# Gated linear recurrence and gated feed-forward on one core: one output projection step moved to the head of the later log passes

## The chip, the cores and the metric

The kernel runs on one core of a Trainium2 chip. The metric is the device time of one execution in microseconds (us); the median of 5 runs before the change is 286.07 us (284.23 to 286.88).

## The reference

Inputs q, k, v, a_re, a_im have shape (4, 8, 768, 48): batch, heads, sequence, head width. A complex decay (a_re, a_im), its magnitude held below 0.999, drives a recurrence; its real output y becomes the 3072 x 384 matrix x of a gated feed-forward.

```
S_re, S_im = (ar * S_re - ai * S_im + k v^T, ar * S_im + ai * S_re)
y[t] = q[t] @ S_re
...
g = x @ w_gate;  val = x @ w_val
ffn_out = (gelu(g) * val) @ w_out
out = x + sigmoid(x @ w_res) * ffn_out
```

w_gate and w_val are 384 x 1536, w_out is 1536 x 384, w_res is 384 x 384.

## The kernel before, in words

**Tiles and units.** The sequence is cut into 12 groups of 256 rows (two chunks of 128 rows, c = 0 and 1, all 8 heads, 384 columns). The groups g are numbered with the batch innermost, so groups 0 to 3 start the four sequences. They form seven units: [0], [1,2], [3,4], [5,6], [7,8], [9,10], [11]. A unit of two groups has 512 rows.

**Phases.** After a ramp (units 0 and 1 prepared), an outer loop over u calls `phase_x(u)`, here called log pass u, for u > 0, then `residuals()`, then `phase_y(u)`, then the loads for later units. Counted from u = 0, the passes with u >= 2 are "from the third on".

- *Log pass u* does, for the groups of unit u+1, the cumulative sums of the log magnitudes on TensorE (`cs_l`, matmuls of L272 named csl, float32), their exponentials E and Ei on ScalarE (L275, L276; reported as L144, the line of the helper `act`), the phase sums (`cs_t`, L291 and L293, named cst) with their reduction on VectorE (L295, L296, L301), and sines on ScalarE (`p2_sin`). For unit u+2 it does logarithms, exponentials (their product with a_im is L254 on VectorE) and arctangents. `decay2` sends rows of E and Ei through DRAM by GpSimd's queue (L345, L349, and L316 back); `multiply` (L361, VectorE, in phase y) makes of them the state's decay. Changes of ScalarE's function table are loads of their own (L642). It also holds the second half of the attention of unit u, and the output projection of unit u-1: one `op_step` per 128 rows, so four of them for a unit of two groups.
- *Phase y(u)* does the gate and value matmuls of unit u (`gv_step`, L595 gp and L599 vp, 12 steps), Gelu on ScalarE, the product of the two on VectorE (L602, into the tile h2), the residual gate (`rp_step`, L611), the products of the next unit's q and k with E and Ei and the sines (`products`, L369, L374, L381), and from its sixth tenth on the first half of the attention of unit u+1.

**Attention.** From group 3 on (`TURN`) Q and K are turned by transposing DMAs on SyncE's queue (L385, QT and KT). One attention step multiplies KT with QT (L446, named at), VectorE masks it (L449, atm), further steps are dk (L488), the state update and y (L496, L498), ScalarE casts y to x (L501), and `xt_step` transposes x on TensorE (L580, tpx).

**op_step (L615 to L631).** Twelve accumulating matmuls (L619) over the 12 slices of h2 into one PSUM tile; VectorE multiplies it with the residual gate into ot (L625); SyncE's queue writes ot to the output (L629). Later `residuals()` adds x to it by an accumulating DMA on GpSimd's queue (L637). A step needs all of h2, thus the last Gelu product of the phase y before.

**What sets the order.** `weave` gives each step of a stream a place between the stream's two ends (0 is the pass's start, 1 its end) and emits the steps in the order of these places. That is the program order; it becomes priority: a compile-time scheduler may issue a later step ahead of an earlier one that it takes to be not ready. On the chip each engine runs its instructions in the order so fixed, and each waits for its own semaphores. SyncE's queue takes, in this order around a pass: the transposes of the phase y before, then the loads of q, k, a_re, a_im for later units, then the writes of ot, then the next transposes.

**PSUM.** The pool psM has four one-bank buffers with one tag for csl, cst, op, gp, vp, rp and tpx, so at most four of these live at a time.

Of the kernel before, what the change touches and what calls it, by code (L numbers as in the profile page):

```python
# [17 lines left out]
def weave(*streams):  # L18

    order = []  # L20
    for si, (begin, end, steps) in enumerate(streams):
        n = len(steps)
        for i, step in enumerate(steps):
            order.append((begin + (end - begin) * (i + 0.5) / n, si, i, step))
    for _, _, _, step in sorted(order, key=lambda e: e[:3]):
        step()
# [3 lines left out]
def kernel(  # L30
# [181 lines left out]
    def squares(g):  # L212

        def q0():
            T["lm", g] = pS.tile([128, W], FP, tag="s", name="lm")
            with paced("gelu"):
                nc.scalar.activation(out=T["lm", g], in_=flat(T["ar", g]), func=AF.Square)

        def q1():
            if g < 5:  # L220
                if g == 0:
                    T["sq"] = hb.tile([128, 4, 2, DM], FP, tag="h2", name="sq0")
                t = T["sq"][:, g % 4].rearrange("p a m -> p (a m)")
            else:
                t = pE.tile([128, W], FP, tag="E", name="sq")
            T["sq", g] = t
            if g in DVSQ:
                nc.vector.tensor_tensor(out=t, in0=flat(T["ai", g]), in1=flat(T["ai", g]), op=OP.mult)
            else:
                with paced("gelu"):  # L230
                    nc.scalar.activation(out=t, in_=flat(T["ai", g]), func=AF.Square)  # L231

        def q2():
            with paced("gmul"):
                nc.vector._custom_dve(TENSOR_ADD_SAT, out=T["lm", g], in0=T["lm", g], in1=T["sq", g], s0=MAG2MAX, s1=0.0)  # L235
            if g in UNITS[2]:
                decay_raw(g)
        return [q0, q1, q2]

    def p1_steps(g):  # L240

        def s0():
            lm = T["lm", g]
            act(out=lm, in_=lm, func=AF.Ln)

        def s1():
            ar = flat(T["ar", g])
            T["s", g] = pE.tile([128, W], FP, tag="E" if g == 1 else "Ei", name="ra") if g in (1, 2) else ar
            act(out=T["s", g], in_=ar, func=AF.Ln)

        def s2():
            T["th", g] = flat(T["ai", g])
            act(out=T["s", g], in_=T["s", g], func=AF.Exp, scale=-1.0)
            nc.vector.tensor_tensor(out=T["th", g], in0=T["s", g], in1=T["th", g], op=OP.mult)  # L254
        return [s0, s1, s2]
# [5 lines left out]
    def cs_l(g, c):  # L261
        if c == 0:
            if g == 0:
                t = hb.tile([128, 4, DM], FP, tag="sg", name="E0")
                T["E", g] = t[:, 0:2].rearrange("p a m -> p (a m)")
                T["Ei", g] = t[:, 2:4].rearrange("p a m -> p (a m)")
            else:
                T["E", g] = pE.tile([128, W], FP, tag="E", name="E")
                T["Ei", g] = pE.tile([128, W], FP, tag="Ei", name="Ei")
        sl = slice(c * DM, (c + 1) * DM)  # L270
        cs = psM.tile([128, DM], FP, tag="mm", padded_shape=[128, 512], name="csl")
        nc.tensor.matmul(out=cs, lhsT=lmat[c], rhs=T["lm", g][:, sl], start=True, stop=True)  # L272

        def ex():
            act(out=T["E", g][:, sl], in_=cs, func=AF.Exp, scale=0.5)  # L275
            act(out=T["Ei", g][:, sl], in_=cs, func=AF.Exp, scale=-0.5)  # L276
        return ex
# [362 lines left out]
    def table(nm):  # L640
        def f():
            tab(nc.scalar.preload_act_table_set(nm))  # L642
        return f

    def gs(u):
        return UNITS[u] if 0 <= u < NU else []
# [7 lines left out]
    def call(f, *a):  # L654
        return lambda: f(*a)

    def zip_steps(lists):
        return [st[i] for i in range(max(map(len, lists), default=0)) for st in lists if i < len(st)]

    def att_steps(u, half):  # L660

        todo = [(g, c, i * C + c) for i, g in enumerate(gs(u)) for c in range(C)]
        n = len(todo) // 2
        steps = []
        for i, (g, c, jj) in enumerate(todo[half * n:half * n + n]):
            steps += attention(g, c)
            if i > 0:
                steps.insert(-1, call(xt_step, u, jj - 1))
        if n:
            steps.append(call(xt_step, u, half * n + n - 1))  # L670
        return steps

    def phase_x(u):

        pend = []
        g1 = gs(u + 1)
        p1g = [g for w in range(NU) if P1AT.get(w, w - 2) == u for g in gs(w)]
        now = [g for g in p1g if g in g1]
        ahead = [g for g in p1g if g not in g1]
        ops = [call(op_step, u - 1, jj) for jj in range(len(gs(u - 1)) * C)]  # L680
        att = att_steps(u, 1)
        if not g1:
            weave((0.0, 0.8, att), (0.1, 1.0, ops))
            return

        def csl(g, c):
            pend.append(cs_l(g, c))

        def ex():
            pend.pop(0)()  # L690

        def p1(g):
            st = p1_steps(g)[1:] if u < LAZY else p1_steps(g) + [call(decay0, g)]
            return (squares(g) if g == HELD else []) + st
        lns = [f for g in g1 for f in (p1_steps(g)[0], call(decay_exp, g))] if u <= LAZY else []
        csls = [call(csl, g, c) for g in g1 for c in range(C)]
        exs = [ex for _ in g1 for _ in range(C)]
        dec = [call(decay2, g) for g in g1]
        cst = [call(cs_t, g, c) for g in g1 for c in range(C)]
        sin = [call(p2_sin, g) for g in g1]  # L700
        table("natural_log_exp_and_others")()
        if now:
            atn = [table("trig_and_small")] + [call(p1_arctan, g) for g in now + ahead]
            pn = zip_steps([p1(g) for g in now])
            weave((0.0, 0.05, pn[:2]), (0.06, 0.1, csls), (0.12, 0.25, pn[2:]), (0.26, 0.4, exs),
                  (0.28, 0.48, zip_steps([p1(g) for g in ahead])),
                  (0.5, 0.5, dec), (0.55, 0.65, atn), (0.62, 0.8, cst), (0.9, 0.95, sin),
                  (0.0, 0.8, att), (0.0, 0.25, ops) if u == 1 else (0.1, 1.0, ops))
            return
        atn = [table("trig_and_small")] + [call(p1_arctan, g) for g in ahead]  # L710
        weave((0.0, 0.1, lns), (0.06, 0.16, csls) if lns else (0.0, 0.12, csls), (0.05, 0.5, zip_steps([p1(g) for g in ahead])), (0.12, 0.45, exs),
              (0.46, 0.46, dec), (0.2, 0.65, cst), (0.7, 0.95, atn + sin), (0.0, 0.8, att), (0.1, 1.0, ops))

    def ramp():

# [101 lines left out]
    for u in range(NU + 1):  # L817
        if u > 0:
            phase_x(u)
        if u == 1:  # L820
            with paced("turned"):
                for g in UNITS[3]:
                    decay_raw(g)
        residuals()
        phase_y(u)
        for g in gs(u + 2):
            with paced("turn"):
                load_q(g)
            after_landing(T["k", g], call(load_v, g))
        while T["a"] < (8 if u == 0 else min(NG, gs(u + 1)[-1] + 7 if gs(u + 1) else NG)):  # L830
            with paced("turn"):
                load_a(T["a"])
# [30 lines left out]
```

## Time and profile before

The profile is of one execution, whose own time was 286.39 us; its span on the core is 284.6 us, so 1.8 us lie around the span.

| what | measured |
|---|---|
| median of 5 runs, range | 286.07 us, 284.23 to 286.88 |
| profiled execution, its span | 286.39 us, 284.6 us |
| busy, TensorE / VectorE / ScalarE / GpSimd | 86% / 76% / 70% / 33% |
| L619 op: matmuls, busy | 288 (24 steps of 12), 50.7 us |
| L272 csl: idle of TensorE before it, in all | 11.4 us |
| log pass 2 (csl to the first gp) | about 107.1 to 126.0 us |
| log passes 3, 4, 5 begin their csl at | 147.0, 187.7, 225.2 us |
| write of one ot: KB, issue to landing | 192.0, 3.2 us |

Durations of single matmuls in the profile are latencies; twelve op matmuls in a row take 1.95 us on the chain (326 ns is the latency of one). "Idle" is the time an engine stood still before an instruction, with who ended the wait. PEclk is the granted share of TensorE's clock.

### The profile page before, as it was taken

The page shows a single profiled execution, that of the slowest core. Times are in us where ns is not written, and L with a number is a line of the kernel's source. Part 1 is how long each engine was busy: PE and PEld are TensorE (multiplying, and loading weights), DVE is VectorE, ACT ScalarE, POOL GpSimd, SP SyncE. Part 2 cuts the span into 40 slices and gives each one's busy share as a digit, 9 for nine tenths or more (in the row PEclk, how much of TensorE's full clock was granted, in tenths as well). Part 3 has the DMA queues.
Part 4 walks back from the last instruction along what each step waited for, and adds up shares of the span by engine and source line. Part 5 has one row for each costly group of instructions (what it writes and reads, how often), then busy time and mean ns, then how long its engine had stood idle before and what let it go on. Part 6 is the DMA issues. An engine that isn't in the chain of part 4 may idle for free.

```text
span 284.6 us, 5133 instructions
## 1 busy us (share of the span) xinstructions
PE 244.8 (86%) x1848; PEld 147.3 (52%) x1848; DVE 215.0 (76%) x376; ACT 198.8 (70%) x336; POOL 93.7 (33%) x141
## 2 busy tenths in 40 slices
PE   0435967997879969999999999989999998999993
PEld 0122645775434446554566544656545665456782
DVE  0669896995999575998878998869968587564453
ACT  4886898579994699885789866696655735455250
POOL 4021843130246402446604476024911242100220
PEclk9977586999999998999999999999999999999999
DMA  9999999999999999999999999999699486900631
GB/s 147 187 173 189 165 191 189 175 160 188 195 170 209 165 198 170 174 198 176 198 170 169 174 156 195 168 171 77 102 201 217 87 89 126 165 20 28 140 55 56
DMA packets 176001, 44.01 MB, mean 155 GB/s; under 512 B 165092, under 2 KB 175976, under 8 KB 175976
## 3 DMA queue, kind: packets, MB, share of 16 engines
q1 hardware_dynamic: 140744, 33.05, 70.6%
q0 software_dynamic: 35232, 10.64, 36.8%
q8 instruction: 14, 0.23, 0.3%
q14 instruction: 11, 0.09, 0.2%
HBM read 31.33 MB, written 9.08 MB: 142 GB/s over the span
## 4 chain that ended last, share of the span: by engine, by line
PE 64%; DMA 14%; DVE 7%; ACT 6%; SPq 5%; issue 2%; DVEq 0%
PE op L619 14%; PE gp L595 13%; PE vp L599 13%; DMA KT<-padK 8%; PE cst L291 5%; PE csl L272 5%; DMA q<-in_q_dram 5%; SPq L164 4%; PE at L446 2%; PE rp L611 2%; DMA ai<-in_a_im_dram 2%; PE tpx L580 2%; PE cst L293 2%; PE dk L488 1%; SPq L385 1%
## 5 line engine op out<-in xcount | busy, mean ns | idle before, releaser
L144 ACT ACTIVATE h<-gp 128x512 bf16<-128x512 f32 (+1 forms) x84 | 44.7, 536 | 38.1 <-PE gp L595 37.8
L602 DVE SCALAR_TENSOR_TENSOR h<-h,vp 128x512 bf16<-128x512 bf16 (+1 forms) x84 | 50.5, 608 | 20.3 <-PE vp L599 13.0
L595 PE MATMUL gp<-xT,wg 128*128 128x512 bf16 (+1 forms) x252 | 61.4, 352 | 1.5 <-ACT h L144 1.1
L599 PE MATMUL vp<-xT,wv 128*128 128x512 bf16 (+1 forms) x252 | 61.8, 352 | 0.5 <-ACT xT L584 0.4
L619 PE MATMUL op<-wo,h 128*128 128x384 bf16 x288 | 50.7, 326 | 1.4 <-ACT xT L584 1.3
L619 PEld LDWEIGHTS <-h 128*128 128x128 bf16 x288 | 27.3, 98 | 18.7 <-issue 2.5
L599 PEld LDWEIGHTS <-wv 128*128 128x128 bf16 x252 | 24.7, 99 | 22.9 <-issue 0.6
L316 POOL DMA_DIRECT2D m<-d x32 | 23.7, 778 | 37.1 <-DMA d<-Ei 17.1
L637 POOL DMA_DIRECT2D out_dram<-x x22 | 20.4, 1022 | 40.4 <-DMA out_dram<-ot 40.2
L595 PEld LDWEIGHTS <-wg 128*128 128x128 bf16 x252 | 23.6, 99 | 18.8 <-issue 1.7
L449 DVE TENSOR_TENSOR atm<-at,mask 128x512 bf16<-128x512 f32 x36 | 24.6, 684 | 8.8 <-PE at L446 8.8
L178 POOL DMA_DIRECT2D v<-in_v_dram x24 | 21.9, 919 | 17.7 <-DMA ai<-in_a_im_dram 12.2
L642 ACT ACT_TABLE_LOAD x21 | 26.9, 1283 | 1.1 <-PEq L847 0.7
L201 POOL COPY landed<-k 1x1 f32<-1x1 f32 x9 | 2.4, 267 | 64.3 <-DMA k<-in_k_dram 64.3
L272 PE MATMUL csl<-lm,lt0a 128*128 128x384 f32 x24 | 13.1, 637 | 11.4 <-ACT lm L144 11.4
L625 DVE SCALAR_TENSOR_TENSOR ot<-sg,op 128x384 f32<-128x384 f32 x24 | 13.2, 549 | 8.6 <-PE op L619 5.7
L291 PE MATMUL cst<-ai,ut0b 128*128 128x384 f32 x40 | 17.8, 537 | 0.1
L446 PE MATMUL at<-QT,KT 96*128 96x128 bf16 x144 | 14.4, 220 | 3.2 <-DMA KT<-padK 2.7
L235 DVE CUSTOM_DVE_ANT_0 lm<-lm,sq 128x768 f32<-128x768 f32 x12 | 11.4, 950 | 7.4 <-ACT sq L231 7.4
L144 ACT ACTIVATE ar<-ar 128x768 f32<-128x768 f32 x20 | 16.9, 851 | 0.1
L501 ACT CAST x<-y 128x384 bf16<-128x384 f32 x22 | 10.5, 478 | 8.9 <-PE y L498 8.5
L144 ACT ACTIVATE sg<-rp 128x384 f32<-128x384 f32 x24 | 11.6, 491 | 6.5 <-PE rp L611 5.4
(113 smaller groups left out, 459.1 us busy)
## 6 DMA issues: line engine op xcount, KB each, us to landing
ar<-in_a_re_dram SPq DMA_DIRECT2D x24, 192.0 KB, 5.0
ai<-in_a_im_dram SPq DMA_DIRECT2D x24, 192.0 KB, 5.0
q<-in_q_dram SPq DMA_DIRECT2D x24, 192.0 KB, 4.8
k<-in_k_dram SPq DMA_DIRECT2D x24, 192.0 KB, 5.1
out_dram<-ot SPq DMA_DIRECT2D x24, 192.0 KB, 3.2
out_dram<-x POOLq DMA_DIRECT2D x22, 192.0 KB, 5.6
v<-in_v_dram POOLq DMA_DIRECT2D x24, 96.0 KB, 5.1
wg<-in_moe_w_gate_dram POOLq DMA_DIRECT2D x4, 288.0 KB, 7.4
```

Source lines behind the costliest of these rows:

```text
L144: return tab(nc.scalar.activation(**kw))
L178: held(nc.gpsimd.dma_start(out=t[:, c], in_=rows(v, g, c)), after)
L272: nc.tensor.matmul(out=cs, lhsT=lmat[c], rhs=T["lm", g][:, sl], start=True, stop=True)
L291: nc.tensor.matmul(out=cs, lhsT=tmat[c if s == 0 else 1], rhs=th[:, sl], start=True, stop=(s == 0 or c == 0))
L316: T["turned"] = nc.gpsimd.dma_start(out=m[u * D:(u + 1) * D].rearrange("p r h -> p (r h)"), in_=md.rearrange("r (h d) -> d (r h)", h=H))
L449: nc.vector.tensor_tensor(out=atm, in0=at, in1=mask4, op=OP.mult)
L595: nc.tensor.matmul(out=gp, lhsT=wg[:, fi, ffi * 128:(ffi + 1) * 128], rhs=xT[:, fi, :], start=(fi == 0), stop=(fi == KD - 1))
L599: nc.tensor.matmul(out=vp, lhsT=wv[:, fi, ffi * 128:(ffi + 1) * 128], rhs=xT[:, fi, :], start=(fi == 0), stop=(fi == KD - 1))
L602: T["gmul"] = nc.vector.scalar_tensor_tensor(out=h2[:, ffi, :], in0=h2[:, ffi, :], scalar=0.5, in1=vp, op0=OP.mult, op1=OP.mult)
L619: nc.tensor.matmul(out=ps, lhsT=h2[:, ffi, jj * 128:(jj + 1) * 128], rhs=wo[:, ffi, :], start=(ffi == 0), stop=(ffi == KF - 1))
L637: nc.gpsimd.dma_start(out=out[t0:t0 + 128, :], in_=x, accum_op=OP.add)
L642: tab(nc.scalar.preload_act_table_set(nm))
```

## The change

In log passes with u >= 2 the four op steps are no longer spread evenly from 0.1 to 1.0. The first gets the place 0.0, ahead of all other steps of the pass; the other three are spread from 0.3 to 1.0. The four places go from 0.2125, 0.4375, 0.6625, 0.8875 to 0.0, 0.4167, 0.65, 0.8833. Log pass 1 and the last two passes (6 and 7, which have no log work and return earlier) keep their order, so the edit acts in passes 2, 3, 4 and 5.

```diff
@@ -709,7 +709,8 @@
             return
         atn = [table("trig_and_small")] + [call(p1_arctan, g) for g in ahead]
         weave((0.0, 0.1, lns), (0.06, 0.16, csls) if lns else (0.0, 0.12, csls), (0.05, 0.5, zip_steps([p1(g) for g in ahead])), (0.12, 0.45, exs),
-              (0.46, 0.46, dec), (0.2, 0.65, cst), (0.7, 0.95, atn + sin), (0.0, 0.8, att), (0.1, 1.0, ops))
+              (0.46, 0.46, dec), (0.2, 0.65, cst), (0.7, 0.95, atn + sin), (0.0, 0.8, att),
+              *([(0.1, 1.0, ops)] if u < 2 else [(0.0, 0.0, ops[:1]), (0.3, 1.0, ops[1:])]))
```

## The prediction

> **What bounds the kernel now.** I read the page first, then the chain of waits in the stretch 99 to 130 us, then the same stretch as a table of windows, then the timelines of each engine at the heads of passes 2 to 5.
>
> The page: TensorE is busy 86% of the span, and the chain that ended last is 64% TensorE. The clock is full from pass 2 on except for one slice.
>
> ```profile
> PE 244.8 (86%) x1848; PEld 147.3 (52%) x1848; DVE 215.0 (76%) x376; ACT 198.8 (70%) x336; POOL 93.7 (33%) x141
> ...
> PEclk9977586999999998999999999999999999999999
> ```
>
> So only TensorE's holes matter, as long as VectorE and ScalarE follow. The chain around the head of pass 2 (start, duration, what):
>
> ```profile
> 99.71 6.10 DMA KT<-padK
> 105.82 0.05 issue
> 105.86 0.57 PE at L446 x4
> 106.43 0.60 PE dk L488 x8
> 107.03 0.32 PE tpx L580 x3
> 107.35 2.40 PE csl L272 x4
> ...
> 112.48 1.95 PE op L619 x12
> ```
>
> TensorE waits for group 4's KT until 105.82, although h2 is complete (last L602 ends at 102.55), and does the first op step only at 112.48. The windows of that stretch (time, PE busy, PEld, DVE, ACT, POOL, clock, DMA share, GB/s):
>
> ```profile
> 102.54:105.95 3.41, 0.89 (x13) 0.40 (x12) 2.55 (x7) 3.38 (x6) 0.00 (x0) 1.00 1.34 177
> 105.95:109.37 3.42, 3.42 (x19) 2.46 (x20) 1.51 (x3) 3.36 (x9) 0.00 (x0) 0.50 1.43 187
> ```
>
> After the hole the clock is halved for 3.42 us, just under csl. The other heads, from their timelines (start, duration, instruction, idle before):
>
> ```profile
> 185.58 0.20 PE L496 MATMUL y<-v,atm 128*128 128x48 bf16 x1 [0.41 <-DVE atm L449]
> ...
> 186.96 0.38 PE L446 MATMUL at<-QT,KT 96*128 96x128 bf16 x4 [0.43 <-DVE atm L449]
> 187.54 0.34 PE L580 MATMUL tpx<-ident,x 128*128 128x128 bf16 x3 [0.20 <-ACT x L501]
> ...
> 190.64 0.96 DVE L369 TENSOR_TENSOR q<-q,E 128x768 bf16<-128x768 f32 x1 [2.30 <-ACT E L144]
> ```
>
> Pass 4 has 1.04 us of holes at its head, and VectorE starts its backlog only when E is there. Passes 3 and 5 have next to none (0.22 us before dk at 150.75 in pass 3).
>
> **The change, part by part.** Nothing is added or removed: 4 x 12 matmuls, 4 L625 and 4 writes move. Steps 2 to 4 of each pass move by 0.004 to 0.02 of a pass; step 2 passes one at step of four matmuls (0.22 us), nothing else on TensorE. I cost these at nothing. The stalls at the passes' ends (0.58, 0.57, 0.57, 0.89 us, tpx for the cast x, with op step 4 behind it) stay.
>
> *Pass 2, TensorE.* With the highest priority of the pass, step 1 can run as soon as h2 is whole and the older work of phase y is out: y ends at 103.56, so the step runs 103.6 to 105.5, inside the 2.28 us wait for KT. at, dk and tpx follow at 105.86 as before. That takes 1.95 us out of the path behind csl. [...] By the row, a window with 0.89 of 3.41 us busy was followed by one at 0.50, a loss of 3.42 x 0.5 = 1.7 us of TensorE time. I go with the row: with 2.84 us busy the window should stay full, and TensorE is offered 1.95 + 1.7 = 3.65 us.
>
> *Pass 2, what is late next.* ScalarE is busy without a break from 103.66 to 116.09 and does not depend on csl's speed there (E begins at 109.37, right behind a logarithm, csl of that chunk was done by 108.7). VectorE idles 3.16 us before L449 at 111.36, which waits for the at matmuls stuck among the slow csl; from there to 128.7 it has no break but 0.21 us. A full clock starts that run at most 1.1 us earlier (q*E at 112.45 needs the second E and Ei, ended 111.3 and 111.7); step 1's L625 (0.55 us) goes into the idle time before; the 0.21 us wait for op goes: 1.86 us. The second L254 (116.93) needs ScalarE's exponential that ends at 115.24: 1.7 us at most. Without the clock effect it is 0.76 us. The pass ends by VectorE (L301), sine, table load (1.28 us), first Gelu at 127.61; all of that moves with VectorE. I take 1.7.
>
> *Queues.* Each op step brings one write on SyncE's queue. In pass 2 that queue issues loads until 122.62, then three writes until 124.92, then QT at 125.79, which waited for padQ. Step 1's write, ready 9 us sooner, still sits behind the loads, so no load waits for it; but QT can come only 0.84 us sooner. Its cost is bounded by where KT is used: group 5's KT landed at 136.55 for an at at 137.38, slack 0.83, so 0.83 + 0.84 covers 1.67 us. Group 6's KT landed at 146.53 for an at at 146.57: no slack, but that at opens pass 3, where the moved step of pass 3 now stands ahead of it and fills up to 1.95 us. GpSimd's queue gets its accumulating write earlier by no more than the landing; its decay transfers hang on loads and do not move: group 6's landed at 136.37 for L361 at 137.28, slack 0.9. VectorE, 1.7 early, would wait 0.8 us there, in phase y where it idles 0.6 us in each 1.3 us Gelu step; I charge 0.3. Pass 2 nets 1.4 us, between 0.5 (VectorE gains 0.76, part lost at L361) and 1.9.
>
> *Pass 3.* No holes to fill but 0.22 us. csl comes up to 1.1 us later relative to the rest, but ScalarE is busy with the table load and logarithms until 149.9, so E hardly moves. One L625 leaves VectorE's full stretch. Gain 0.1, between -0.3 and 0.5.
>
> *Pass 4.* Step 1 covers the 1.04 us of holes; csl is then 1.95 - 1.04 = 0.9 us later, and so is E, which waited 0.39 us for csl already. VectorE's run from 190.64 to the last L301 at 202.77 has no break; it starts up to 0.9 later and is 0.55 shorter (L625 goes into the idle 2.30). The last sine, the table load and the first Gelu (ending 206.94) gate the third gp at 207.09. So TensorE's gain of up to 1.04 cannot pass: between +1.0 and -0.4; I take 0, near the VectorE row, which ends last.
>
> *Pass 5.* No hole. E, at 226.65, comes about 1.2 us later; VectorE's idle time later (0.73 us before L295 at 233.79, which waits for cst) and the L625 moved out (0.55) cover it. If not, 0.5 is lost. I take 0.
>
> *Sum.* 1.4 + 0.1 + 0 + 0 = 1.5 us. The profiled execution took 286.39 (span 284.6 plus 1.8 around it): 284.9. It stands 0.3 above the median, so against 286.07 the time is 284.6.
>
> **The rivals.**
>
> *A: the holes of pass 4 are paid too.* If VectorE's order lets L295 and L301 move ahead of the q and k products, pass 4 gives its 1.04 and pass 3 its 0.5: about 3.0 us, 283.1. For it: cst follows csl directly, without an op step between. Against it: VectorE has no break there.
>
> *B: nothing comes through.* The gain of pass 2 is given back at L361 (transfers of GpSimd's queue) and at group 5's KT: DMA engines are busy throughout until about 206 us, and landings may not move at all. Then 286.1, within 0.5 either way.
>
> *C: slower, the lead step pushes csl back.* Its place is the queue of TensorE at the head of each pass. If the scheduler takes h2 to be ready after KT, step 1 stands behind the at of 105.86: nothing is filled, its twelve matmuls run mostly at half clock (105.86 plus 1.15 us of at, dk, tpx, then 7 of 12 until 109.37), csl starts at 110.2 instead of 107.35, and E at 110.9 instead of 109.37: 1.5 us on ScalarE's unbroken run, less 0.55 from L625: 0.9. The same push gives 0.4 in pass 4 and 0.5 in pass 5: 1.8 us, 287.9. It decides at one point: whether the step's first matmul starts before or after group 4's KT has landed (105.82). Against it: the older y steps end at 103.56 in the trace and h2 is whole by 102.55, so any estimate near these durations puts the step first.
>
> **How the numbers follow.** My forecast (in sum a gain of 0.5 to 2.4) has 0.48, A 0.15, B 0.15, C 0.22. About 0.5% (1.4 us) is what a measurement can tell from no change. A bit over half of the forecast's chance lies beyond it: faster 0.26 + 0.15 = 0.41; same 0.22 + 0.15 = 0.37; slower 0.22. The range: low end 282.4, just under A with pass 2 at its 1.9 (286.07 - 1.9 - 0.5 - 1.04 = 282.6); high end 287.6, into C, leaving out the most of C and a little beyond A, under 0.2 together.
>
> **What would show it.** Right: L619 in TensorE's timeline between y and group 4's at, the wait for KT down from 2.28 to about 0.3, clock 1.00 at 106 to 109, the first Gelu of phase y(2) about 1.5 us sooner, L619 ahead of group 6's at. Wrong: L619 between at and csl in pass 2, a half clock still there, new idle time at L361 or at group 5's KT as large as the gain, E in pass 4 or 5 later with the third gp waiting for Gelu.

## The result, and the profile after

The change makes the kernel a little faster: 285.32 us in the median of 44 runs (283.98 to 287.62) against 286.15 us of the kernel before in runs beside it; the ratio is 0.9979 (95% interval 0.9965 to 0.9993). That is 0.6 us or 0.2%, where 1.5 us or 0.5% was forecast: right in sign, 0.4 of the size. Ratios here and below are taken from fast executions alone, a few being in a slower state, and are not the quotients of the medians given (these stand 0.83 us apart).

The profiled execution after took 284.67 us, span 282.8. Its first and second part of the page, TensorE's row and its granted clock:

```profile
PE 242.9 (86%) x1848; PEld 145.9 (52%) x1848; DVE 214.7 (76%) x376; ACT 198.7 (70%) x336; POOL 93.4 (33%) x141
...
PEclk9999786999999998999999999999999999999999
```

Busy shares are as before, and one slice of the clock still falls short in the middle. The two profiles differ by 1.87 us at the end, but 0.88 of that is there when phase y(1) issues its last gp (100.03 before, 99.15 after), ahead of all that the change touches. To read the change, each log pass has to be taken by itself, from the end of the last gp of the phase y ahead of it to the first gp of the next:

| log pass, us | before | after | difference | TensorE idle in it, before and after |
|---|---|---|---|---|
| 2 | 25.64 | 25.12 | -0.52 | 3.33, 2.90 |
| 3 | 21.58 | 21.19 | -0.39 | 0.87, 0.59 |
| 4 | 21.89 | 22.00 | +0.11 | 1.61, 1.60 |
| 5 | 17.57 | 17.50 | -0.07 | 0.89, 0.99 |

The head of pass 2 in TensorE's timeline of the kernel after (start, duration, instruction, idle before it and its releaser):

```profile
102.52 0.18 PE L498 MATMUL y<-Gb,QT 96*128 96x48 bf16 x1
104.04 0.40 PE L446 MATMUL at<-QT,KT 96*128 96x128 bf16 x4 [1.34 <-DMA KT<-padK]
104.27 0.50 PE L488 MATMUL dk<-v,padK 128*96 128x48 bf16 x8
104.61 0.34 PE L580 MATMUL tpx<-ident,x 128*128 128x128 bf16 x3
104.79 3.74 PE L619 MATMUL op<-wo,h 128*128 128x384 bf16 x12
108.32 0.90 PE L272 MATMUL csl<-lm,lt0a 128*128 128x384 f32 x2
```

The step was to fill the wait for KT. It stands behind that wait, behind at, dk and tpx, and right ahead of csl. The windows of the same stretch (time; busy of PE, PEld, DVE, ACT, POOL; clock, DMA share, GB/s) show that the half clock has not gone either; it now slows the step, which takes 3.74 us and not 1.95, instead of csl:

```profile
101.70:105.10 3.40, 1.82 (x28) 1.22 (x26) 3.14 (x8) 3.37 (x6) 0.00 (x0) 1.00 0.99 194
105.10:108.50 3.40, 3.40 (x13) 1.82 (x11) 0.79 (x3) 3.34 (x9) 0.32 (x2) 0.50 1.37 191
108.50:111.90 3.40, 3.40 (x15) 1.92 (x14) 1.03 (x2) 2.72 (x7) 1.61 (x2) 1.00 1.68 183
```

In pass 4 it is the same order, and the three holes that the step was to cover stay in front of it:

```profile
183.80 0.20 PE L496 MATMUL y<-v,atm 128*128 128x48 bf16 x1 [0.41 <-DVE atm L449]
...
185.19 0.38 PE L446 MATMUL at<-QT,KT 96*128 96x128 bf16 x4 [0.43 <-DVE atm L449]
185.76 0.34 PE L580 MATMUL tpx<-ident,x 128*128 128x128 bf16 x3 [0.19 <-ACT x L501]
185.94 2.11 PE L619 MATMUL op<-wo,h 128*128 128x384 bf16 x12
187.89 0.81 PE L272 MATMUL csl<-lm,lt0a 128*128 128x384 f32 x2
```

In all four passes the step sits between the last tpx of the phase y before and csl. That is the fact to explain. ScalarE's timeline at the head of pass 2 tells what that tpx waits for:

```profile
102.25 0.51 ACT L144 ACTIVATE sg<-rp 128x384 f32<-128x384 f32 x1
102.78 1.28 ACT L642 ACT_TABLE_LOAD   x1
104.08 0.48 ACT L501 CAST x<-y 128x384 bf16<-128x384 f32 x1
...
109.26 0.49 ACT L144 ACTIVATE E<-csl 128x384 f32<-128x384 f32 x1 [0.68 <-PE csl L272]
```

tpx needs the cast x, which stands behind a table load. And E, which in the kernel before followed a logarithm without a wait, now waits 0.68 us for the csl behind the step.

### The profile page after: what moved, and what is told of

Read it like the earlier page. It is cut to its first block, busy times and chain, and to the rows that moved or that the text cites. A ratio compares the mean times of both kernels' runs of the same rounds, so it can differ in the third digit from the quotient of the medians.

```text
span 282.8 us, 5144 instructions
## 1 busy us (share of the span) xinstructions
PE 242.9 (86%) x1848; PEld 145.9 (52%) x1848; DVE 214.7 (76%) x376; ACT 198.7 (70%) x336; POOL 93.4 (33%) x141
## 4 chain that ended last, share of the span: by engine, by line
PE 66%; ACT 14%; DVE 7%; DMA 5%; SPq 3%; issue 3%; DVEq 0%
PE gp L595 16%; PE vp L599 15%; PE op L619 13%; PE csl L272 5%; PE cst L291 4%; SPq L164 3%; PE rp L611 3%; ACT L642 3%; ACT CS L144 3%; PE at L446 2%; DMA KT<-padK 2%; DMA ai<-in_a_im_dram 2%; PE dk L488 2%; PE tpx L580 1%; ACT ar L144 1%
## 5 line engine op out<-in xcount | busy, mean ns | idle before, releaser
L619 PE MATMUL op<-wo,h 128*128 128x384 bf16 x288 | 52.7, 333 | 1.4 <-ACT xT L584 1.3
L637 POOL DMA_DIRECT2D out_dram<-x x22 | 21.0, 1093 | 43.8 <-DMA out_dram<-ot 43.8
L625 DVE SCALAR_TENSOR_TENSOR ot<-sg,op 128x384 f32<-128x384 f32 x24 | 13.2, 548 | 15.0 <-PE op L619 12.2
L201 POOL COPY landed<-k 1x1 f32<-1x1 f32 x9 | 1.7, 186 | 61.8 <-DMA k<-in_k_dram 61.8
L272 PE MATMUL csl<-lm,lt0a 128*128 128x384 f32 x24 | 11.4, 562 | 11.6 <-ACT lm L144 11.4
L144 ACT ACTIVATE E<-csl 128x384 f32<-128x384 f32 x26 | 12.6, 492 | 5.2 <-PE csl L272 4.5
```

Source lines behind the costliest of these rows:

```text
L144: return tab(nc.scalar.activation(**kw))
L619: nc.tensor.matmul(out=ps, lhsT=h2[:, ffi, jj * 128:(jj + 1) * 128], rhs=wo[:, ffi, :], start=(ffi == 0), stop=(ffi == KF - 1))
L637: nc.gpsimd.dma_start(out=out[t0:t0 + 128, :], in_=x, accum_op=OP.add)
```

## The experiments

Two theories went into the first experiments. *Order*: tiles of psM appear on TensorE in program order, so that nothing that uses psM can pass the tpx emitted before it; the place 0.0 is then not early enough. *Readiness*: the compile-time scheduler takes the step's h2 to be ready only after KT. A third question was which passes the 0.6 us come from.

### 1 and 2. Pass 2 alone, passes 3 to 5 alone

```diff
-              *([(0.1, 1.0, ops)] if u < 2 else [(0.0, 0.0, ops[:1]), (0.3, 1.0, ops[1:])]))
+              *([(0.1, 1.0, ops)] if u != 2 else [(0.0, 0.0, ops[:1]), (0.3, 1.0, ops[1:])]))
```

The second kernel has `u < 3` there.

> The change in pass 2 alone. Theory A (the step stands behind the transposes tpx that end phase y, which wait for ScalarE's cast, so the wait for KT stays and the step runs at half clock in csl's place): no hole is filled, E is about 1 us later, L625 leaves VectorE's run: within 0.5 us of before (ratio 0.998 to 1.002). Theory B (the whole gain sits in pass 2, small because of landings): 0.998, as the full change. In the profile A wants the idle time before group 4's at as before, and op matmuls at about double spacing right after it.

> The change in passes 3, 4 and 5 without pass 2. Theory A: pass 3 gives about 0.4 us (step 1 off the middle of a pass with two full engines), passes 4 and 5 nothing: ratio 0.9985, between 0.997 and 1.0. Theory B: 1.000.

Measured: 0.9946 (0.9925 to 0.9966) for pass 2 alone, 0.9982 (0.9963 to 1.0001) for passes 3 to 5. In its profile the second gives passes 3, 4 and 5 as 21.20, 22.00 and 17.50 us, the lengths of the kernel after within 0.01: together 0.34 us less than before. Pass 2 alone came out below the whole change, which no sum of parts explains. Its profiled execution had KT early: the wait was 0.31 us, the clock stayed full, and the pass took 23.62 us. The wait for KT ends with a transfer's landing and differs from one execution to the next, for programs that are the same up to there: 2.28 us (before), 1.94 (passes 3 to 5 alone), 1.22 (experiment 5, below), all three with the old order of pass 2; 1.34 (after).

### 3 and 4. The step emitted ahead of the last tpx

The step is emitted in phase y(1), at 0.975 of it, ahead of the tpx at 0.983; the other three keep the places of the change. Then the same for the steps of passes 2 to 5.

```diff
-        ops = [call(op_step, u - 1, jj) for jj in range(len(gs(u - 1)) * C)]
+        ops = [call(op_step, u - 1, jj) for jj in range(len(gs(u - 1)) * C)][int(u - 1 in (1,)):]
...
+              (0.3, 1.0, ops) if u - 1 in (1,) else (0.1, 1.0, ops))
...
+        , *([(0.975, 0.975, [call(op_step, u, 0)])] if u in (1,) else []))
```

> Step 1 of pass 2 alone is emitted still earlier, in phase y(1) between its last residual gate step and its last xt_step, so that it comes ahead of the transposes in TensorE's order; steps 2 to 4 as in the change; other passes as before. Theory A: the wait for KT falls to about 0.3 us, no half clock in 100 to 112 us, and the gain that the prediction gave pass 2 appears: 1.0 to 1.7 us, ratio 0.994 to 0.9965. Theory B (landings at L361 and group 5's KT take it back anyway): no better than the change, 0.998 to 1.0.

> The same for passes 2 to 5: every first step ahead of the last transposes of the phase y before. Theory A: pass 2 as in the run of pass 2 alone, and pass 4's holes (1.04 us) are covered, of which little comes through because VectorE's run ends last: ratio 0.992 to 0.996. Theory B: 0.998, as the change.

Measured: 1.0019 (0.9994 to 1.0045) and 1.0019 (0.9997 to 1.0041): no gain at all, though the heads of the passes did what the prediction hoped for. In the first, TensorE runs the step from 101.21 to 103.6, waits for KT not at all, and keeps its full clock; pass 2 takes 22.88 us, 2.8 less than in the profile before. In the second, pass 4 falls from 21.89 to 20.93 as well. But phase y(2), from its first to its last gp, grows from 17.15 to 22.0 and 21.7 us. VectorE's timeline of the first kernel there:

```profile
132.63 0.69 DVE L602 SCALAR_TENSOR_TENSOR h<-h,vp 128x512 bf16<-128x512 bf16 x1 [0.61 <-PE vp L599]
133.24 0.16 DVE L361 TENSOR_TENSOR M<-m 96x8 f32<-96x8 f32 x1
136.73 0.16 DVE L361 TENSOR_TENSOR M<-m 96x8 f32<-96x8 f32 x1 [3.34 <-DMA m<-d]
```

and TensorE's, which stops for want of atm:

```profile
138.25 0.58 PE L446 MATMUL at<-QT,KT 96*128 96x128 bf16 x4 [2.97 <-DVE atm L449]
```

VectorE arrives at the second L361 (group 6) before its transfer has landed, and everything behind it waits: the masks, the Gelu products, and then TensorE for 2.97 us, after which its clock is halved for 3.4 us (three gp matmuls take 1.48 us at 138.62 and 0.81 at 133.56; some 1.7 us of work). Those two make 4.7 of the 4.9 us. Counted from the last gp of y(1), VectorE comes to this L361 2.4 us earlier than before (34.95 against 37.33 us), and the transfer lands 1.9 us later (38.20 against 36.34), which together use up about 1 us of slack and leave the wait. GpSimd's timeline shows what stood in front of the transfer:

```profile
117.56 0.92 POOL L637 DMA_DIRECT2D out_dram<-x  x1 [2.60 <-DMA out_dram<-ot]
118.14 0.84 POOL L345 DMA_DIRECT2D d<-Ei  x1
118.66 0.81 POOL L349 DMA_DIRECT2D d<-E  x1
123.42 1.51 POOL L316 DMA_DIRECT2D m<-d  x2 [3.95 <-DMA d<-Ei]
...
131.65 1.50 POOL L316 DMA_DIRECT2D m<-d  x2 [5.24 <-issue]
```

With the step this early, the compiled order has its accumulating write (L637) at the front of GpSimd's queue, though the program still emits it behind the log pass. It waits there 2.60 us for ot to land, and the decay rows stand behind it. Their last transfer (the second of the x2 at 131.65) lands at 136.64. That this write made the transfer late is likely but not shown: no run moved it by itself, and a row's time from issue to landing differs between executions too (124.92 to 130.63 here, 126.26 to 129.28 before).

### 5 to 8. The second L361 moved late

To see whether this stall is all that eats the gain, the L361 of the second group of y(2) is moved from the middle to the end of the phase: alone, with experiment 3, with the steps of passes 2, 3 and 4 early (pass 5 as in the change), and with the change itself. The edit in short (for u = 1 the place stays 0.9 to 0.95):

```diff
-(0.55, 0.56, dec3)
+*([(0.55, 0.56, dec3)] if u != 2 else [(0.55, 0.55, dec3[:1]), (0.95, 0.95, dec3[1:])])
```

> The kernel before, with one VectorE step moved: in phase y(2) group 6's L361 is emitted at 0.95 of the phase, not right behind group 5's at 0.55. Control for the next runs. Before, group 6's transfer had landed 0.9 us ahead of L361, so neither theory sees a difference: 0.998 to 1.002.

> Pass 2's first step ahead of the last transposes, and group 6's L361 late. Theory A (in the run without this, pass 2 became 2.8 us shorter and phase y(2) 4.9 us longer, because VectorE stood at group 6's L361 until its transfer landed at 136.7): the stall of 3 us at the at matmuls of 138 us goes, phase y(2) is again about 17.2 us from first to last gp, and 1.5 to 2.7 us of gain reach the end: ratio 0.990 to 0.995. Theory B (the DMA stream itself sets when phase y(2) can end, another landing comes next): 0.998 to 1.002.

> The same in passes 2, 3 and 4; pass 5 as in the change; group 6's L361 late. Theory A: to pass 2's gain come 0.5 us of pass 3 and 0.9 us of pass 4 (the holes before the last transposes are filled; their lengths in the run with all four were 21.0 and 20.9 us against 21.6 and 21.9): ratio 0.985 to 0.991. Theory B: only passes 3 and 4 count, 0.995.

> The change, with group 6's L361 late. In the change's own profile VectorE did not wait at L361, so theory A sees no difference to the change: 0.996 to 0.999. Were L361 what the change's small gain is lost to, it would be 0.994 or less.

Measured: alone 1.0005 (0.9983 to 1.0028); with experiment 3 0.9910 (0.9875 to 0.9944); with three early steps 0.9858 (0.9819 to 0.9897), 282.87 us beside 286.63, below both kernels of this case; with the change 0.9992 (0.9964 to 1.0021). So the move is worth nothing where nobody is early, and where the step fills the hole it gives back what was lost: y(2) is 17.38 us in both profiles. In experiment 6 it is the step of pass 2 alone that gains 2.6 us (1.6 to 3.6). Pass 4 of the kernel with three early steps, TensorE:

```profile
183.16 0.65 PE L619 MATMUL op<-wo,h 128*128 128x384 bf16 x3
...
183.95 1.62 PE L619 MATMUL op<-wo,h 128*128 128x384 bf16 x9
185.69 0.34 PE L580 MATMUL tpx<-ident,x 128*128 128x128 bf16 x3
185.87 0.86 PE L272 MATMUL csl<-lm,lt0a 128*128 128x384 f32 x2
```

No idle time is named in these rows: the holes of 0.41, 0.43 and 0.20 us are filled, and the pass is 0.96 us shorter. In this execution 1.48 us are lost again at the same L361 one phase later, in y(3).

### 9 and 10. The change word for word, the step in another bank

The step keeps its place, 0.0 of the log pass. Only its PSUM tile comes from the one bank of the pool psT, which no csl, gp, vp, rp or tpx uses. If *readiness* sets the order, the step stays where it is; if *order* does, it moves ahead of tpx.

```diff
-        ps = psM.tile([128, DM], FP, tag="mm", padded_shape=[128, 512], name="op")
+        own = jj == 0 and 1 <= u <= 4; ps = (psT if own else psM).tile([128, DM], FP, tag="tp" if own else "mm", padded_shape=[128, 512], name="op")
```

The second kernel has the late L361 of experiment 5 as well.

> The change word for word, but the first op step of passes 2 to 5 writes the PSUM bank of the pool psT, idle after group 2, and not one of psM's four. Theory A (psM's four buffers are handed out in program order, so the step can't pass the last tpx of phase y): with its own bank the step goes ahead of tpx with no change of place, pass 2 becomes 22.8 us long, no half clock at 102 to 112 us, and VectorE then stands at group 6's L361: ratio 1.000 to 1.004, as in the run with the steps emitted early. If the pool's order is not the cause, it is as the change, 0.997 to 0.999.

> The same with group 6's L361 late. Theory A: as the run with early steps and late L361, 0.984 to 0.990. Else 0.998.

Measured: 0.9943 (0.9914 to 0.9971) and 0.9931 (0.9902 to 0.9960). TensorE's head of pass 2 in the first:

```profile
103.50 0.49 PE L619 MATMUL op<-wo,h 128*128 128x384 bf16 x2
...
104.12 1.78 PE L619 MATMUL op<-wo,h 128*128 128x384 bf16 x10
106.19 0.34 PE L580 MATMUL tpx<-ident,x 128*128 128x128 bf16 x3 [0.28 <-ACT x L501]
106.36 0.39 PE L446 MATMUL at<-QT,KT 96*128 96x128 bf16 x4
...
106.93 0.91 PE L272 MATMUL csl<-lm,lt0a 128*128 128x384 f32 x2
```

and the window over it (columns as above):

```profile
104.40:107.80 3.40, 3.12 (x27) 2.04 (x25) 2.91 (x6) 3.36 (x7) 0.00 (x0) 1.00 1.25 209
```

This settles what held the step: with nothing changed but the bank, it leaves the tpx behind, fills the wait, and the clock stays at 1.00. It was the shared pool, and not h2. How the pool does it is not shown. On the chip no buffer was lacking in the kernel after: h2 was whole at 101.67, and the tiles of psM ahead of the last tpx had all been read by 102.76 (rp by ScalarE, the line at 102.25 above), yet the step began at 104.79. So it was the order fixed at compile time; whether that comes from handing out the buffers in program order, or from the scheduler's own estimate of when one is free, no run here tells.

Passes 2, 3 and 4 take 22.79, 21.15 and 20.93 us, in all 4.2 us less than in the profile before.

The stall in y(2) that was expected of the first did not come, and GpSimd's queue shows why:

```profile
117.14 0.53 POOL L345 DMA_DIRECT2D d<-Ei  x1
117.65 0.52 POOL L349 DMA_DIRECT2D d<-E  x1
...
130.01 1.50 POOL L316 DMA_DIRECT2D m<-d  x2 [4.37 <-DMA d<-Ei]
```

Here the step is still emitted in the log pass, no L637 stands ahead of the decay rows, and the transfer lands at 134.46, a microsecond before VectorE's L361 at 135.43. It is y(3) that loses time in this execution, at the same place of VectorE's order:

```profile
176.17 0.16 DVE L361 TENSOR_TENSOR M<-m 96x8 f32<-96x8 f32 x1 [1.98 <-DMA m<-d]
```

y(3) takes 18.79 us instead of 17.08, and y(2) and pass 5 are 0.2 us longer each; this leaves 2.1 us, beside a ratio that stands for 1.6 (0.8 to 2.5). The repeat of pass 2 alone (experiment 12), whose pass 3 is that of the kernel before, also waited 1.93 us at this place, so the landings alone can do it. The second kernel missed its forecast too. Its profiled execution is the shortest of all (span 280.7) and has no such wait; its median is 284.93 us. What its other executions lose, their profiles were not there to tell: that stays open.

### 11 and 12. The change and pass 2 alone, once more

Neither kernel is changed; this asks how far one kernel's ratio can be trusted.

> The change once more, beside the runs with an own bank on one chip, and beside pass 2 alone: 0.9965 to 0.9995.

> The change in pass 2 alone once more; it came out at 0.9946, better than the whole change (0.9979), though passes 3 to 5 were 0.4 us shorter with the change in the traces. If that was spread between chips, it is now no better than the change beside it: 0.997 to 1.001. If the change in pass 2 gives 1.5 us by itself, 0.995 again.

Measured: 0.9987 (0.9962 to 1.0011) and 0.9972 (0.9953 to 0.9991). The change's ratio of 0.9979 lies in both intervals. The repeat of the change cannot be told from no change. So pass 2 alone is not shown to beat the whole change, and the 0.9946 of experiment 1 may have been partly chance; passes 3, 4 and 5 of the repeated change are 21.20, 22.00 and 17.50 us again. The profile of pass 2 alone also held a surprise, in TensorE's timeline:

```profile
105.45 0.40 PE L446 MATMUL at<-QT,KT 96*128 96x128 bf16 x4 [1.88 <-DMA KT<-padK]
...
106.20 2.11 PE L619 MATMUL op<-wo,h 128*128 128x384 bf16 x12
```

After a wait of 1.88 us, longer than the 1.34 us of the kernel after, the step ran at full clock.

## Why the prediction was wrong in size, step by step

*Pass 2, TensorE: the step that failed.* "With the highest priority of the pass, step 1 can run as soon as h2 is whole and the older work of phase y is out: y ends at 103.56, so the step runs 103.6 to 105.5, inside the 2.28 us wait for KT." The last tpx belonged to the older work too. It waits for ScalarE's cast x (before: 104.96 to 105.44, behind a table load), and the step shares the pool psM with it. In the kernel after, y ended at 102.70 and the step ran from 104.79 to 108.5 behind at, dk and tpx: after the wait, and slowed by the half clock. The profile before held the evidence: ScalarE's timeline shows the cast, TensorE's shows tpx at 107.03, after KT. Experiment 9 shows by the bank alone that the shared pool held the step. It also refutes the reason that rival C gave for its order, that h2 might be taken to be ready after KT.

*The size of that gain* was not overstated. Where the step does fill the hole, pass 2 takes 22.79 to 23.09 us in six profiles, against 24.24 to 25.64 in three with the old order: 1.2 to 2.8 us shorter, where 1.7 was the sum behind VectorE. TensorE's offer of 3.65 us holds for an execution like the one before; the half clock in it comes in two of those three.

*The clock.* The prediction went by one row, with 0.89 of 3.41 us busy ahead of the half clock. The runs sharpen it. Half clock followed waits for KT of 2.28, 1.94, 1.53 and 1.34 us; with 1.88 us (experiment 12), 1.22 and 0.31 us the clock stayed full. The length of the wait does not decide it. In the profiles before and after the changes of the clock lie whole multiples of 3.413 us apart (before: 1, 2, 1, 2, 2, 2, 17, 1 and 51; after: 2, 1, 2, 2, 17, 1 and 51), so they can be put on a grid; in experiments 2 and 11 the half clock of pass 2 lasted 3.4 us too. Where the grid lies differs from one execution to the next; in experiments 5 and 12, whose clock did not change between 96 and 113 us, its place there is the author's estimate. TensorE's busy time in a window of the grid can then be held against the clock in the next:

| profile | wait for KT, us | window of the grid | busy in it, us | clock in the next |
|---|---|---|---|---|
| before | 2.28 | 102.53 to 105.94 | 0.89 | half |
| experiment 2 | 1.94 | 101.07 to 104.49 | 1.42 | half |
| experiment 11 | 1.53 | 101.64 to 105.06 | 1.64 | half |
| after | 1.34 | 101.67 to 105.09 | 1.83 | half |
| experiment 12 | 1.88 | 101.45 to 104.86 | 1.89 | full |
| experiment 5 | 1.22 | 103.97 to 107.38 | 2.06 | full |

By that estimate the wait of 1.88 us lies across a border of the grid, at 104.86 (the two windows of experiment 12, columns as above):

```profile
101.45:104.86 3.41, 1.89 (x29) 1.13 (x25) 3.41 (x8) 3.39 (x6) 0.00 (x0) 1.00 1.08 206
104.86:108.27 3.41, 2.81 (x28) 2.11 (x29) 1.66 (x4) 3.37 (x8) 0.00 (x0) 1.00 1.21 196
```

From 46 us on the profiles before and after hold 136 windows at full clock, 68 each. After all 132 with 2.07 us of work or more it stayed full. After the other four it halved: the two of the table, 0.89 and 1.83 us, and one with 0.30 and one with none at the end of the execution. Ahead of 46 us the work in a window alone does not part them: in the profile after, the clock stayed full after 0.37 us (12.93 to 16.34) and 1.82 us (23.17 to 26.58) and halved after 1.90 us (36.82 to 40.24). What else it goes by, no run here shows.

*Pass 2, what really happened.* The step displaces csl, as rival C said: E starts 0.77 us later, counted from the last gp of y(1) (109.26 - 99.15 against 109.37 - 100.03). C reckoned 1.5, less 0.55 for the L625 that leaves VectorE's run: 0.9. The pass is 0.52 us shorter all the same, with KT 0.94 us less late in this execution, a difference that kernels with the old order show among themselves (waits of 1.22 to 2.28 us). "The stalls at the passes' ends ... stay" failed as well: in pass 2 the last tpx waits 1.32 us for the cast x and not 0.58, in all five profiles with this order in pass 2 (1.32 to 1.33 us). TensorE gets there 1.26 us earlier (counted as above), the cast only 0.5: between sines, ScalarE sets its time. What the change is worth in pass 2 by itself cannot be told from these runs, since KT's landing and the half clock move the pass by more than a microsecond from one execution to the next: it took 25.64, 25.18 and 24.24 us with the old order, 25.12, 25.30, 23.62 and 23.97 with the new one (and 27.38 in experiment 8's profile, an execution of 288.62 us).

*Pass 3* was reckoned at 0.1 (between -0.3 and 0.5) and gave 0.39. The hole of 0.22 us before dk (a wait for VectorE's Gb) and one of 0.08 us at KT are gone; about 0.1 stays unassigned. It is the same in three profiles. *Pass 5*: 0 forecast, 0.07 found.

*Pass 4*: 0 forecast, 0.11 lost, so the forecast held, but for a wrong reason. The prediction held that TensorE's gain "cannot pass" VectorE's run without a break. When the holes are really filled, 0.96 of 1.04 us pass (experiments 4, 7 and 9), as rival A said. The term that was wrong is that run, which was taken to keep its order and to be 0.55 us shorter. VectorE's end of it before (the first two lines) and after:

```profile
200.98 0.95 DVE L381 TENSOR_TENSOR padQ<-CS,q 128x1536 bf16<-128x1536 bf16 x1
202.77 0.55 DVE L301 TENSOR_SCALAR ai<-lm 128x768 int32<-128x768 int32 x1
...
200.54 0.56 DVE L301 TENSOR_SCALAR ai<-lm 128x768 int32<-128x768 int32 x1
201.35 0.95 DVE L381 TENSOR_TENSOR padQ<-CS,q 128x1536 bf16<-128x1536 bf16 x1
```

From its first product with E to its last L301 the run took 12.13 us before (from 190.64) and 9.79 after (from 190.75), because L301 now comes ahead of products that stood in front of it, which is what A named as its condition. So it could start 1.88 us later in the pass (10.29 against 8.41 us after the last gp) and the pass grew by only 0.11. In the change itself nothing passes since nothing is filled.

*L361 and GpSimd's queue.* The prediction named the right place (slack 0.9 us at L361) and charged 0.3 us for a gain of 1.7. Where the gain came, the charge was up to 4.9 us: VectorE does not merely idle there, as all of its later work and TensorE's stand behind one small transfer. And "its decay transfers hang on loads and do not move" did not hold where the step was emitted in phase y: its accumulating write came ahead of them there, and rival B's give-back came true in experiments 3 and 4.

*Rival C* had the order in all four passes and named the point at which it decides. Its price failed: it gave 1.8 us in all, of which passes 4 and 5 were to lose 0.4 and 0.5, and they changed by +0.11 and -0.07. So the change neither fills a hole nor does harm; the gain that comes back in each profile is that of passes 3 to 5: 0.35 us, and 0.34 in experiments 2 and 11.

## What to carry to other kernels

A place in the program order is not yet a place on the engine: before counting on a hole, list what the moved step shares with work that is emitted ahead of it, PSUM buffers above all, and ask what that work waits for. Then go on to the next wait in order: an engine that arrives earlier can run into a transfer whose slack was enough until then, and pay more than it gained (experiment 3: 2.8 us gained in pass 2, 4.9 lost in y(2)). To prove an order, change the shared resource and leave the place alone.

## What the runs showed of the hardware that was not expected

- TensorE's clock changed on a grid of 3.413 us in the profiles before and after. From 46 us on it fell to one half after the four windows of this grid with 1.83 us of work or less and stayed full after the 132 with 2.07 us or more; earlier in the kernel after it stayed full after 1.82 us and fell after 1.90. A half clock followed a wait of 1.34 us inside one window (after), and none a wait of 1.88 us with 1.89 and 2.81 us of work in the two windows that it lies in (experiment 12, border by estimate).
- Transfers of 1.5 and 3 KB through DRAM on GpSimd's queue took 3.0 to 7.4 us from issue to landing between 112 and 146 us of the kernel before (126.26 to 129.28, 138.40 to 145.84). In experiment 3 VectorE came 2.4 us earlier to one that landed 1.9 us later, stood 3.34 us, and TensorE behind it 2.97 us.
